# Two batches' scores in one turn of TensorE, two batches' outputs and states in another, and the score tiles' diagonals moved from GpSimd to ScalarE

## The chip, the cores and the metric

One core of a Trainium2 chip runs the whole program. The engines are TensorE (PE; its weight loads are PEld), VectorE (DVE), ScalarE (ACT), GpSimd (POOL) and SyncE (SP), which here issues nearly all DMAs. The metric is the device time of one execution in microseconds (us); lower is better.

## The reference

```python
B, H, S, D = 4, 8, 768, 48
for t in range(S):
    kt, vt, rt = k[:, :, t], v[:, :, t], r[:, :, t]
    cur = np.einsum('bhd,bhe->bhde', u[None] * kt, vt)
    y[:, :, t] = np.einsum('bhd,bhde->bhe', rt, state + cur)
    state = w[None, :, :, None] * state + np.einsum('bhd,bhe->bhde', kt, vt)
x = y.transpose(0, 2, 1, 3).reshape(B * S, H * D)          # 3072 tokens x 384
x = (silu(x @ w_gate) * (x @ w_val)) @ w_out               # inner width 1536
h = x @ w_in                                               # inner width 2048
return (h * np.tanh(np.log1p(np.exp(h)))) @ w_out2
```

A decaying linear attention is followed by two feed-forward networks (FFNs). Everything is float32.

## The kernel before, in words

**Blocks, units, places.** The 768 tokens are cut into six blocks j = 0 to 5 of 128 tokens, each for 4 batches b. The first FFN works on all 4 batches of a block at once (512 columns) in units n = 0 to 71; a unit is one block and one slice f of 128 inner features, and has three groups of nine 128x512 matmuls: `gate`, `val` and `out` (the helper on L294 issues them all, as a high part and a low part of each operand). `out` belongs to the unit before. The table `UNITS` gives the order within a unit; from unit 24 on it is "gate fill act val mul tick mine fill out fill tick tick". `act` is ScalarE's silu of `gate` (L723), `mul` VectorE's product with `val` (L727), `hi` ScalarE's rounded copy (L729), `mine` VectorE's remainder (L735). A `tick` is one step of rounding weights: L180 and L228 on ScalarE, L188, L194, L206 and L212 on VectorE, and L234 on VectorE for the first 36 tiles and on GpSimd for the others. A `fill` is a place where a piece of attention work may be put; each unit has three.

**Attention from block 2 on.** For one batch of one block: GpSimd multiplies r by k and by u (`first` L502, `second` L504), VectorE sums it per head (`total`, L510), and GpSimd writes these sums onto the diagonals of the two score tiles (`diag`, L515: two operations on 128x512). GpSimd also scales r and k by powers of the decay (`later`, `sooner`, L477) and the untransposed k (`keys`, L524). TensorE makes the scores (`scores`, L534, 8 matmuls into two PSUM banks), VectorE copies what lies above the diagonal over them into the two score tiles (`mask`, L541). TensorE then makes the output (`out`, L583, 28 matmuls) and the block's contribution to the state (`state`, L616, 8 matmuls); ScalarE and VectorE round the output into x (`hi` L652, `low` L662), ScalarE fades the state (L639) and VectorE adds to it (`sum`, L632). I call such a run of attention matmuls between FFN matmuls a turn. One batch has two turns, one of scores and one of outputs and states.

**What sets the order.** The lists `AHEAD`, `BEGIN`, `STEPS` and `SPREAD` give the parts in order, and `beside` says at which unit a list begins; a `Filler` deals its steps out over the places. The number behind a part says how many batches ahead it is. Units 14 to 18 still round weights that they need at once. Attention of block 2 lies in units 18 to 23, of blocks 3, 4 and 5 beside units 24 to 59. Within one engine the instructions run in program order.

**Buffers.** `ps_mm` has two PSUM banks, taken in turn by `gate` and `val`; so `gate` of a unit waits until `act` of the unit before has read the same bank. `ps_at` has three, taken in turn by scores (two), output (one) and state (one). `apool` holds two batches of r, k, v; the tile `pr` of `first` and `second` exists once, so `first` waits for the `total` of the batch before. The score tiles exist once.

Of the kernel before, what the change touches and what calls it, by code (L numbers as in the profile page):

```python
# [8 lines left out]
F32 = mybir.dt.float32  # L9
# [3 lines left out]
ALU = mybir.AluOpType  # L13
# [3 lines left out]
P = 128  # L17
# [64 lines left out]

EDGE = 352


@with_exitstack
def tile_decay_attention_then_two_ffns(
# [229 lines left out]
    ypool = first.enter_context(tc.tile_pool(name="ypool", bufs=1))  # L317
    epool = first.enter_context(tc.tile_pool(name="epool", bufs=1))
# [89 lines left out]

    scores = [spool.tile([P, NPAIR, CH], F32, name=f"s{g}") for g in range(2)]
    for t in scores:  # L410
        nc.vector.memset(t, 0.0)
    powers = NPAIR * (HALF + 1)
    pw, qw = ypool.tile([P, DM], F32, name="y"), epool.tile([P, DM], F32, name="pr")
    ones = pw[:, powers : powers + HALF]
# [26 lines left out]
    w128 = const.tile([P, NPAIR], F32, name="w128")  # L441
    late = apool.tile([P, 2, ROW], F32, name="rkv_sb")[:, 0, :WIDE]
    late = late.rearrange("p (n t) -> p n t", n=NPAIR)
    second = apool.tile([P, 2, ROW], F32, name="rkv_sb")
    other = second[:, 1, :WIDE].rearrange("p (n t) -> p n t", n=NPAIR)
    second = second[:, 0, :DM]
    tabn = const.tile([P, H, D], F32, name="tabn")
# [63 lines left out]

    def at_diagonal(j, b):

        for g in range(2):
            nc.gpsimd.tensor_tensor(  # L515
                out=scores[g], in0=four(ident),
                in1=at_in[j, b]["sums"][:, g::2, :].to_broadcast([P, NPAIR, CH]), op=ALU.mult,
            )

# [45 lines left out]

    def at_turned(a, b, ps):


        a["turned"] = ps
        todo = [  # L570
            (i, m, state[:, b, i, m * QUAD : (m + 1) * QUAD], a["r"][:, i, :])
            for m in range(3) for i in range(NPAIR)
        ]
        for g, places in enumerate((((0, 0), (1, QUAD)), ((2, 2 * QUAD + PD - D), (1, QUAD + PD - D)))):
            todo += [
                (i, m, a["v"][i // 2][:, i % 2, c : c + QUAD], scores[g][:, i, :])
                for m, c in places for i in range(NPAIR)
            ]
        ends = {(3 * i + m) % 4: n for n, (i, m, _, _) in enumerate(todo)}
        begun_q = set()  # L580
        for n, (i, m, lhsT, rhs) in enumerate(todo):
            c, q = divmod(3 * i + m, 4)
            nc.tensor.matmul(  # L583
                ps[q * QUAD : (q + 1) * QUAD, c, :], lhsT=lhsT, rhs=rhs,
                start=q not in begun_q, stop=ends[q] == n, skip_group_check=True,
            )
            begun_q.add(q)

    def at_mine(j, b):

# [78 lines left out]
    def after(j, b, n):  # L669
# [179 lines left out]
    def unit1(n, fill=nothing, tick=nothing):  # L849
# [52 lines left out]
    for n in range(2, len(units) - NF1):  # L902
        if n in beside:
            fill.flush()
            fill = Filler(*beside[n])
        if n in (2 * PAIRED - 3, 2 * PAIRED - 2):
            ahead = order[EARLY * B + n - 2 * PAIRED + 3]
# [619 lines left out]
```

## Time and profile before

| | |
|---|---|
| median of 3 runs | 910.26 us (909.64 to 912.01) |
| the profiled execution | 911.0 us, of which the span from first to last instruction is 909.3 us |
| TensorE matmul busy | 900.7 us, 99% of the span |
| VectorE, ScalarE, GpSimd busy | 614.9, 435.3, 175.2 us |
| 128x512 matmuls of the FFNs | 0.39 us each by the record, one begun every 0.227 us |

Times in the rows below are counted from the first instruction. A matmul's record is longer than its share of the engine, since the next one begins before it ends; so the step from one start to the next is what counts. An instruction's record on VectorE or GpSimd holds the time in which it stood on the engine, also when it was held up there.

### The profile page before, as it was taken

Reading aid. Unit: us, or ns where it says so; the run is one execution under the profiler, and the core shown is the slowest. Engines: PE = TensorE matmul, PEld = TensorE weight load, DVE = VectorE, ACT = ScalarE, POOL = GpSimd, SP = SyncE. Lnnn points to the kernel's source line nnn. Section 1 sums busy time; section 2 is a strip of 40 time slices with the busy share of each in tenths; the row PEclk is TensorE's granted clock in tenths of the full one; section 3 lists DMA queues with packets and bytes.
Section 4 is the critical chain, followed back from the end, with each engine's and each line's share of the span. In section 5 each row is a group of like instructions: output and inputs, shape, how many; then the busy total and the mean of one; then the engine's idle time right before and its main releaser. Section 6 shows DMA issues by size and latency. Waiting matters only on the chain.

```text
span 909.3 us, 14895 instructions
## 1 busy us (share of the span) xinstructions
PE 900.7 (99%) x5625; PEld 735.0 (81%) x5625; DVE 614.9 (68%) x1108; ACT 435.3 (48%) x867; POOL 175.2 (19%) x162
## 2 busy tenths in 40 slices
PE   9999999999999999999999999999999999999998
PEld 6888887778888878888888888888888888888886
DVE  8898988545778676743224644758876587776587
ACT  5765542323333433421222345756666475665455
POOL 4200103466555555443000100000000000000000
PEclk9999999999999999999999999999999999999999
DMA  8454732425666766541004748977954549645273
GB/s 315 147 152 125 248 120 65 145 102 175 194 219 213 261 205 206 180 149 53 25 0 144 216 139 294 344 253 237 323 191 151 186 151 311 230 142 173 92 232 116
DMA packets 77576, 164.24 MB, mean 181 GB/s; under 512 B 7616, under 2 KB 34624, under 8 KB 77504
## 3 DMA queue, kind: packets, MB, share of 16 engines
q1 hardware_dynamic: 77072, 162.50, 53.7%
q0 software_dynamic: 432, 0.79, 0.5%
q8 instruction: 44, 0.72, 0.3%
q14 instruction: 28, 0.23, 0.1%
HBM read 126.82 MB, written 36.44 MB: 180 GB/s over the span
## 4 chain that ended last, share of the span: by engine, by line
PE 96%; DVE 2%; DMA 0%; ACT 0%; issue 0%; POOL 0%; POOLq 0%; ACTq 0%; DVEq 0%
PE mm L294 40%; PE acc L294 27%; PE at L294 19%; PE at L583 3%; PE at L534 2%; PE mm L534 1%; PE at L560 1%; PE acc L402 1%; PE at L616 1%; PE acc L492 0%; DMA begun<-o 0%; PE at L552 0%; PE at L656 0%; DVE g_lo L735 0%; DVE o L727 0%
## 5 line engine op out<-in xcount | busy, mean ns | idle before, releaser
L294 PE MATMUL mm<-x_hi,w_split 128*128 128x512 f32 x858 | 281.3, 393 | 1.8 <-DVE w_split L234 1.3
L294 PEld LDWEIGHTS mm<-x_hi,w_split 128*128 128x128 f32 x858 | 160.9, 188 | 38.2 <-DVE w_split L234 1.7
L294 PE MATMUL mm<-x_lo,w_split 128*128 128x512 f32 x429 | 167.4, 390 | 0.1
L727 DVE TENSOR_TENSOR o<-mm,o 128x512 f32<-128x512 f32 x72 | 49.7, 690 | 138.0 <-PE mm L294 101.8
L294 PE MATMUL acc<-g_hi,w_split 128*128 128x512 f32 x420 | 141.5, 393 | 0.0
L936 DVE TENSOR_TENSOR g_lo<-g,g_hi 128x512 fp32r<-128x512 f32 x159 | 106.8, 688 | 23.3 <-ACT g_hi L1014 23.0
L729 ACT ACTIVATE g_hi<-o 128x512 fp32r<-128x512 f32 x72 | 45.5, 632 | 130.1 <-DVE o L727 129.7
L294 PE MATMUL acc<-g_hi,v 128*128 128x512 f32 x288 | 105.1, 389 | 0.0
L1014 ACT ACTIVATE g_hi<-g 128x512 fp32r<-128x512 f32 x159 | 96.1, 623 | 18.3 <-PE at L294 16.3
L936 DVE TENSOR_TENSOR g<-g,at 128x512 f32<-128x512 f32 x72 | 49.5, 688 | 71.3 <-PE at L294 42.7
L294 PEld LDWEIGHTS mm<-x_lo,w_split 128*128 128x128 f32 x429 | 80.6, 188 | 16.4 <-DVE x_lo L662 0.4
L294 PEld LDWEIGHTS acc<-g_hi,w_split 128*128 128x128 f32 x420 | 78.8, 188 | 17.5 <-ACT g_hi L729 0.2
L294 PE MATMUL acc<-g_lo,w_split 128*128 128x512 f32 x210 | 82.2, 391 | 0.3 <-DVE g_lo L735 0.3
L723 ACT ACTIVATE o<-mm 128x512 f32<-128x512 f32 x71 | 42.1, 593 | 81.4 <-PE mm L294 66.5
L1213 ACT ACTIVATE g<-g 128x512 f32<-128x512 f32 x72 | 45.5, 632 | 70.2 <-DVE g L936 69.1
L735 DVE TENSOR_TENSOR g_lo<-o,g_hi 128x512 fp32r<-128x512 f32 x72 | 53.9, 749 | 23.7 <-ACT g_hi L729 23.7
L936 DVE TENSOR_TENSOR g<-g 128x512 f32<-128x512 f32 x96 | 64.5, 686 | 2.7 <-ACT g L1213 2.6
L294 PEld LDWEIGHTS acc<-g_hi,v 128*128 128x128 f32 x288 | 54.1, 188 | 11.2
L294 PE MATMUL at<-g_hi,v 128*128 128x512 f32 x192 | 59.6, 389 | 0.0
L294 PE MATMUL acc<-g_lo,v 128*128 128x512 f32 x144 | 56.0, 389 | 0.0
L294 PE MATMUL mm<-b_hi,w_split 128*128 128x512 f32 x144 | 52.1, 389 | 0.0
L294 PE MATMUL at<-b_hi,w_split 128*128 128x512 f32 x144 | 52.1, 389 | 0.0
(170 smaller groups left out, 1499.3 us busy)
## 6 DMA issues: line engine op xcount, KB each, us to landing
w_raw<-w SPq DMA_DIRECT2D x68, 384.0 KB, 3.5
w_split<-w2s SPq DMA_DIRECT2D x48, 384.0 KB, 5.1
rkv_sb<-rkv_t SPq DMA_DIRECT2D x16, 768.0 KB, 5.0
v<-w2a SPq DMA_DIRECT2D x24, 512.0 KB, 4.0
v<-w2b SPq DMA_DIRECT2D x24, 512.0 KB, 3.6
w_split<-w2z SPq DMA_DIRECT2D x24, 384.0 KB, 5.0
n_sb<-rk_n SPq DMA_DIRECT2D x16, 384.0 KB, 5.6
v<-w2c SPq DMA_DIRECT2D x16, 384.0 KB, 3.7
```

The source lines that it names most:

```text
L294: nc.tensor.matmul(acc, lhsT=wt[:, i, sl], rhs=rhs, start=start, stop=stop, skip_group_check=goes_on)
L402: nc.tensor.matmul(idle, lhsT=mask, rhs=mask.rearrange("p (o t) -> p o t", o=1).to_broadcast([P, 4, CH]), start=True, stop=True,)
L534: nc.tensor.matmul(ps[g][:, i, :], lhsT=a["k"][q, i, :], rhs=a["r"][q, i, :], start=True, stop=True,)
L560: nc.tensor.matmul(ps[t, h * D : (h + 1) * D], lhsT=scores[h % 2][:, h // 2, t], rhs=a["v"][:, h, :], start=(j == 0 and h == heads[0]), st ...
L583: nc.tensor.matmul(ps[q * QUAD : (q + 1) * QUAD, c, :], lhsT=lhsT, rhs=rhs, start=q not in begun_q, stop=ends[q] == n, skip_group_check=True,)
L723: nc.scalar.activation(sg, ps, AF.Silu)
L727: nc.vector.tensor_tensor(out=sg, in0=ps, in1=sg, op=ALU.mult)
L729: nc.scalar.activation(hi, sg, AF.Copy)
L735: eng.tensor_tensor(out=lo, in0=sg, in1=f32(hi), op=ALU.subtract)
L936: nc.vector.tensor_tensor(out=o, in0=a, in1=b, op=op)
L1014: nc.scalar.activation(hi, src, AF.Copy)
L1213: nc.scalar.activation(t, t if src is None else src, AF.Mish)
```

## The change

From block 3 on, batches go in pairs. A list `PAIR` of 18 places (six units) holds the two batches' work: `pair` makes the scores of both in one turn (16 matmuls; the first of the four banks is taken from `ps_mm`, since `ps_at` has three), `outs` makes both outputs and then both states in one turn, with one bank for both states. The two batches have score tiles of their own (`masked`). `apool` holds three batches, with room made by a smaller scratch for DMA descriptors, by dropping `ypool` and by using its tiles for the first blocks' y. The diagonals are written by ScalarE, four 128x128 operations with a scale per row for a score tile, in place of one GpSimd operation; this holds for block 2 too, whose batches still go one by one. `AHEAD` and `BEGIN` are rewritten: what block 2's second batch needs is written behind the scores of the first.

```diff
-SPREAD = [
-    "out state load2 diag1", "hi fade keys1", "low", "sum first2", "scores1 second2",
-    "mask1", "total2 later2 sooner2",
+PAIR = [
+    "pair", "odd", "mask1 first2", "second2", "total2 later2", "sooner2", "",
+    "outs load3", "hi hi1 keys2", "low fade", "low1 fade1 first3 load4",
+    "sum second3 deven2", "sum1 later3 dodd2", "total3 sooner3", "keys3", "deven3", "dodd3", "",
 ]
+LAST = ["first2 second2", "total2 later2 sooner2"]
+FIRST = ["deven2", "dodd2 keys2"]
 AHEAD = [
-    [(2, 0, "first second")], [(2, 0, "total later sooner")], [(2, 0, "diag keys")],
-    [(2, 1, "first second")], [(2, 1, "total later sooner")],
+    [(2, 0, "first second")], [(2, 0, "total later sooner")], [(2, 0, "diag")], [(2, 0, "keys")], [],
 ]
-BEGIN = [[(2, 0, "scores")], [(2, 0, "mask")]]
+BEGIN = [
+    [(2, 0, "scores"), (2, 1, "first second later sooner")], [(2, 0, "mask"), (2, 1, "total")],
+]
...
-    apool = first.enter_context(tc.tile_pool(name="apool", bufs=2))
+    apool = first.enter_context(tc.tile_pool(name="apool", bufs=3))
...
+    def at_diagonal(j, b, gs=range(2)):
+
+        for g in gs:
+            for i in range(NPAIR):
+                nc.scalar.activation(
+                    masked[b % 2][g][:, i, :], ident, AF.Copy,
+                    scale=at_in[j, b]["sums"][:, 2 * i + g, :],
+                )
...
+    def at_pair(j, b):
+
+        at_scores(j, b, (ps_mm, "mm"))
+        at_scores(j, b + 1)
+        at_mask(j, b, [0])
+
+    def at_outs(j, b):
+
+        for i in range(2):
+            at_out(j, b + i)
+        if j + 1 < NJ:
+            ps = ps_at.tile([P, 2, NPAIR, D], F32, name="at")
+            for i in range(2):
+                at_state(j, b + i, ps[:, i])
...
-    beside.update({12 * j - 12: (at_steps(j, SPREAD), 34) for j in range(3, NJ)})
+    rest = [[(2, B - 1, step)] for step in FIRST]
+    for pair in order[3 * B :: 2]:
+        rest += [[(*pair, step)] for step in PAIR]
+    beside[24] = (rest, len(rest))
```

The line numbers of the kernel shift by the change; in the pieces below the changed kernel's L188, L236, L525, L669, L682, L757 and L763 are the old L180, L228, the new diagonals, and the old L639, L652, L723 and L729. "x4" behind a row counts operations of one kind in a row, and "waits" names the engines whose semaphores the row waits for.

On ScalarE, from the silu's `hi` of unit 15 to that of unit 16, there stood before (`o<-mm` is the silu, `w_split<-w_num` the last operation of a tick):

```order
L729 ACTIVATE g_hi<-o 128x512 [waits DVE_49]
L180 ACTIVATE w_num<-w_raw 128x384 [waits DMAHW2_49]
L228 ACTIVATE w_split<-w_num 128x384 [waits DVE_49,PE_49]
L723 ACTIVATE o<-mm 128x512 [waits DMAHW5_49,PE_49]
L729 ACTIVATE g_hi<-o 128x512 [waits DVE_49]
```

and there stands after the change:

```order
L763 ACTIVATE g_hi<-o 128x512 [waits DVE_49]
L188 ACTIVATE w_num<-w_raw 128x384 [waits DMAHW4_49]
L236 ACTIVATE w_split<-w_num 128x384 [waits DVE_49,PE_49]
L525 ACTIVATE s_268<-ident,bonus 128x128 x4
L525 ACTIVATE s_269<-ident,bonus 128x128 x4
L757 ACTIVATE o<-mm 128x512 [waits DMAHW7_49,PE_49]
L763 ACTIVATE g_hi<-o 128x512 [waits DVE_49]
```

The eight diagonals of batch (2, 0) now stand between the tick's last operation and the silu of unit 16.

On ScalarE in unit 18, around the first output of block 2 (`x_hi<-at` is its `hi`, `state<-state` the fade), there stood before:

```order
L180 ACTIVATE w_num<-w_raw 128x384 [waits DMAHW1_49,Activation_49]
L228 ACTIVATE w_raw<-w_num 128x384 [waits DVE_49]
L652 ACTIVATE x_hi<-at 128x3x128 [waits PE_49]
L639 ACTIVATE state<-state,w_293 128x96 x4
L723 ACTIVATE o<-mm 128x512 [waits PE_49]
```

and there stands after the change:

```order
L188 ACTIVATE w_num<-w_raw 128x384 [waits DMAHW3_49,Activation_49]
L236 ACTIVATE w_raw<-w_num 128x384 [waits DVE_49]
L525 ACTIVATE s_270<-ident,bonus 128x128 x4
L525 ACTIVATE s_271<-ident,bonus 128x128 x4
L682 ACTIVATE x_hi<-at 128x3x128 [waits PE_49]
L669 ACTIVATE state<-state,w_294 128x96 x4
L757 ACTIVATE o<-mm 128x512 [waits PE_49]
```

The eight diagonals of batch (2, 1) now stand behind the tick and ahead of the `hi` of batch (2, 0).

On GpSimd, from `later` and `sooner` of batch (2, 0) on (`s<-ident,bonus` is a diagonal, `n_sb<-n_sb,tabn` is `keys`, `pr<-n_sb` is `first`), there stood before:

```order
L477 TENSOR_TENSOR rkv_sb<-rkv_sb,tab 128x512 [waits DMAHW1_49]
L477 TENSOR_TENSOR rkv_sb<-rkv_sb,tab 128x512
L515 TENSOR_TENSOR s_271<-ident,bonus 128x512 [waits DVE_49,PE_49]
L515 TENSOR_TENSOR s_272<-ident,bonus 128x512 [waits PE_49]
L524 TENSOR_TENSOR n_sb<-n_sb,tabn 128x384
L502 TENSOR_TENSOR pr<-n_sb 128x384 [waits DMAHW6_49,Pool_49]
L504 TENSOR_TENSOR pr<-pr,u_sb 128x384 [waits Pool_49]
L477 TENSOR_TENSOR rkv_sb<-rkv_sb,tab 128x512 [waits DMAHW5_49,PE_49]
L477 TENSOR_TENSOR rkv_sb<-rkv_sb,tab 128x512
L515 TENSOR_TENSOR s_271<-ident,bonus 128x512 [waits DVE_49,PE_49]
L515 TENSOR_TENSOR s_272<-ident,bonus 128x512 [waits DVE_49,PE_49]
```

and there stands after the change:

```order
L486 TENSOR_TENSOR rkv_sb<-rkv_sb,tab 128x512 [waits DMAHW1_49]
L486 TENSOR_TENSOR rkv_sb<-rkv_sb,tab 128x512
L534 TENSOR_TENSOR n_sb<-n_sb,tabn 128x384
L511 TENSOR_TENSOR pr<-n_sb 128x384 [waits DMAHW6_49,DVE_49]
L513 TENSOR_TENSOR pr<-pr,u_sb 128x384 [waits Pool_49]
L486 TENSOR_TENSOR rkv_sb<-rkv_sb,tab 128x512 [waits DMAHW5_49,PE_49]
L486 TENSOR_TENSOR rkv_sb<-rkv_sb,tab 128x512
L534 TENSOR_TENSOR n_sb<-n_sb,tabn 128x384
L511 TENSOR_TENSOR pr<-n_sb 128x384 [waits DMAHW2_49,DVE_49]
L513 TENSOR_TENSOR pr<-pr,u_sb 128x384 [waits Pool_49]
```

The diagonals, which waited for TensorE, are gone. So `keys` follows at once, and `first` of batch (2, 1) and of batch (2, 2) wait for nothing later than the `total` of the batch before.

## Rows read from the trace of the kernel before

**Rows 1.** The page: busy time, share and instructions of each engine

```profile
PE 900.7 (99%) x5625; PEld 735.0 (81%) x5625; DVE 614.9 (68%) x1108; ACT 435.3 (48%) x867; POOL 175.2 (19%) x162
```

**Rows 2.** Waits of TensorE: waiter <- awaited: us in total, times, longest

```profile
PE mm L294 <- DVE w_split L234: 1.3, 1, 1.3
```

**Rows 3.** TensorE's timeline, one scores turn: start, us, line, operation, shapes, count

```profile
204.57 1.16 PE L534 MATMUL at<-rkv_sb 48*128 48x128 f32 x16
...
204.78 0.95 PE L534 MATMUL at<-rkv_sb 48*128 48x128 f32 x14
...
205.45 0.28 PE L534 MATMUL at<-rkv_sb 48*128 48x128 f32 x2
205.66 0.50 PE L294 MATMUL acc<-g_hi,w_split 128*128 128x512 f32 x1
...
209.65 0.39 PE L294 MATMUL mm<-x_hi,w_split 128*128 128x512 f32 x1
```

**Rows 4.** TensorE's timeline, the turn of output and state that follows

```profile
209.97 0.86 PE L583 MATMUL at<-rkv_sb,state 128*32 128x128 f32 x24
...
211.30 0.40 PE L583 MATMUL at<-s,rkv_sb 128*32 128x128 f32 x8
211.63 0.56 PE L616 MATMUL at<-rkv_sb,n_sb 128*48 128x48 f32 x16
212.13 0.50 PE L294 MATMUL mm<-x_hi,w_split 128*128 128x512 f32 x1
...
214.33 0.40 PE L294 MATMUL acc<-g_hi,w_split 128*128 128x512 f32 x1
...
220.24 0.39 PE L294 MATMUL mm<-x_hi,w_split 128*128 128x512 f32 x1
```

**Rows 5.** Timeline of units 15 and 16: VectorE, GpSimd, ScalarE, TensorE

```profile
135.05 0.55 DVE L510 TENSOR_REDUCE bonus<-pr 128x8 f32<-128x384 f32 x1
137.79 1.52 DVE L735 TENSOR_TENSOR g_lo<-o,g_hi 128x512 fp32r<-128x512 f32 x1 [0.70 <-ACT g_hi L729]
141.23 3.16 POOL L477 TENSOR_TENSOR rkv_sb<-rkv_sb,tab 128x512 f32<-128x512 f32 x2
145.60 0.58 ACT L723 ACTIVATE o<-mm 128x512 f32<-128x512 f32 x1
146.23 0.50 PE L294 MATMUL mm<-x_hi,w_split 128*128 128x512 f32 x1 [0.56 <-ACT o L723]
```

**Rows 6.** Timeline of units 18 and 19 around the first output of block 2

```profile
158.53 1.36 DVE L541 COPY_PREDICATED s<-mask,at 128x512 f32<-128x512 uint16 x2
161.87 0.69 DVE L735 TENSOR_TENSOR g_lo<-o,g_hi 128x512 fp32r<-128x512 f32 x1 [0.70 <-ACT g_hi L729]
163.77 2.48 POOL L515 TENSOR_TENSOR s<-ident,bonus 128x512 f32<-128x512 f32 x2 [19.38 <-DVE w_split L234]
163.95 1.40 DVE L212 SCALAR_TENSOR_TENSOR w_num<-w_raw,w_num 128x384 uint32<-128x384 uint32 x1
165.81 0.47 ACT L652 ACTIVATE x_hi<-at 128x384 fp32r<-128x384 f32 x1
166.32 0.56 DVE L662 TENSOR_TENSOR x_lo<-at,x_hi 128x384 fp32r<-128x384 f32 x1 [0.97 <-ACT x_hi L652]
168.85 1.16 PE L534 MATMUL at<-rkv_sb 48*128 48x128 f32 x16
```

**Rows 7.** GpSimd's timeline where VectorE has no tick: `first`, then `later` and `sooner`

```profile
171.83 1.02 POOL L502 TENSOR_TENSOR pr<-n_sb 128x384 f32<-128x384 f32 x1 [4.60 <-DMA n_sb<-rk_n]
173.90 2.52 POOL L477 TENSOR_TENSOR rkv_sb<-rkv_sb,tab 128x512 f32<-128x512 f32 x2
```

**Rows 8.** ScalarE's timeline: four 128x128 copies with a scale per row

```profile
6.72 1.28 ACT L452 ACTIVATE rkv_sb<-tab,w 128x128 f32<-128x128 f32 x4 [2.90 <-DVE w L450]
```

**Rows 9.** Timeline in a unit of block 3's stage: a silu, and TensorE's next `gate`

```profile
339.68 0.58 ACT L723 ACTIVATE o<-mm 128x512 f32<-128x512 f32 x1
343.09 0.50 PE L294 MATMUL mm<-x_hi,w_split 128*128 128x512 f32 x1
```

More of the change, by code (lines that the diff above doesn't have):

```diff
@@ L46 @@
 STEPS = [
-    "out state load2 diag1", "hi low fade sum keys1", "scores1 first2 second2",
+    "out state load3 diag1", "hi low fade sum keys1", "scores1 first2 second2",
     "mask1 total2 later2 sooner2",
 ]
-SPREAD = [
-    "out state load2 diag1", "hi fade keys1", "low", "sum first2", "scores1 second2",
-    "mask1", "total2 later2 sooner2",
-]
+PAIR = [
[3 rows of a table added]
+]
+LAST = ["first2 second2", "total2 later2 sooner2"]
+FIRST = ["deven2", "dodd2 keys2"]
 KEYS = [[(1, b, "keys")] for b in range(B)]
@@ L83 @@
 EDGE = 352
+SCRATCH = 4096
 @with_exitstack
@@ L407, in tile_decay_attention_then_two_ffns @@
     warm(12)
-    scores = [spool.tile([P, NPAIR, CH], F32, name=f"s{g}") for g in range(2)]
+    masked = [
+        [spool.tile([P, NPAIR, CH], F32, name=f"s{i}{g}") for g in range(2)] for i in range(2)
+    ]
+    scores = masked[0]
     for t in scores:
         nc.vector.memset(t, 0.0)
+    late, second, third = (apool.tile([P, 2, ROW], F32, name="rkv_sb") for _ in range(3))
+    late = late[:, 0, :WIDE].rearrange("p (n t) -> p n t", n=NPAIR)
+    other = second[:, 1, :WIDE].rearrange("p (n t) -> p n t", n=NPAIR)
+    own = [third[:, 0, :DM], second[:, 0, :DM]]
     powers = NPAIR * (HALF + 1)
-    pw, qw = ypool.tile([P, DM], F32, name="y"), epool.tile([P, DM], F32, name="pr")
+    pw, qw = own[0], epool.tile([P, DM], F32, name="pr")
     ones = pw[:, powers : powers + HALF]
@@ L441, in tile_decay_attention_then_two_ffns @@
     w128 = const.tile([P, NPAIR], F32, name="w128")
[L442 to L446, printed above, removed]
     tabn = const.tile([P, H, D], F32, name="tabn")
@@ L510, in at_own @@
             nc.vector.reduce_sum(out=a["sums"], in_=bonus.pop((j, b)), axis=AX.X)
[L512 to L518, printed above, removed]
+    def at_diagonal(j, b, gs=range(2)):
[5 more added lines that the diff above has]
+                )
     def at_keys(j, b):
@@ L524, in at_keys, with at_scores @@
             eng.tensor_tensor(out=kn, in0=kn, in1=tabn, op=ALU.mult)
-    def at_scores(j, b):
+    def at_scores(j, b, first=None):
         a = at[j, b]
-        pool, name = (ps_mm, "mm") if j < EARLY else (ps_at, "at")
-        ps = a["scores"] = [pool.tile([P, 4, CH], F32, name=name) for _ in range(2)]
+        pools = [(ps_mm, "mm") if j < EARLY else (ps_at, "at")] * 2
+        if first:
+            pools[0] = first
+        ps = a["scores"] = [pool.tile([P, 4, CH], F32, name=name) for pool, name in pools]
         for i in range(NPAIR):
@@ L540, in at_mask @@
         for g in gs:
-            nc.vector.copy_predicated(out=scores[g], mask=mask3, data=at[j, b]["scores"][g])
+            to = scores if j < EARLY else masked[b % 2]
+            nc.vector.copy_predicated(out=to[g], mask=mask3, data=at[j, b]["scores"][g])
+    def at_pair(j, b):
[9 more added lines that the diff above has]
+                at_state(j, b + i, ps[:, i])
     def at_out(j, b):
@@ L547, in at_out @@
         if j >= EARLY:
-            return at_turned(a, b, ps[:, :DM].rearrange("p (c t) -> p c t", c=KC))
+            return at_turned(a, b, ps[:, :DM].rearrange("p (c t) -> p c t", c=KC), masked[b % 2])
         if j:
@@ L564, in at_out, with at_turned @@
                 )
-    def at_turned(a, b, ps):
+    def at_turned(a, b, ps, masks):
         a["turned"] = ps
@@ L575, in at_turned @@
             todo += [
-                (i, m, a["v"][i // 2][:, i % 2, c : c + QUAD], scores[g][:, i, :])
+                (i, m, a["v"][i // 2][:, i % 2, c : c + QUAD], masks[g][:, i, :])
                 for m, c in places for i in range(NPAIR)
@@ L591, in at_mine @@
         a = at[j, b]
-        y = a["y"] = second if b % 2 else ypool.tile([P, DM], F32, name="y")
+        y = a["y"] = own[b % 2]
         sums = epool.tile([P, H], F32, name="bonus")
@@ L602, in at_y, with at_state @@
         nc.vector.tensor_tensor(out=a["y"], in0=a["out"][:, :DM], in1=a["y"], op=ALU.add)
-    def at_state(j, b):
+    def at_state(j, b, ps=None):
         if j + 1 == NJ:
@@ L607, in at_state @@
         a = at_in[j, b]
-        if j == 0:
+        if ps is not None:
+            pass
+        elif j == 0:
             ps = ps_acc.tile([P, NPAIR, D], F32, name="acc2")
@@ L682, in tile_decay_attention_then_two_ffns @@
         "mask": at_mask,
-        "even": lambda j, b: at_mask(j, b, [0]),
+        "pair": at_pair,
         "odd": lambda j, b: at_mask(j, b, [1]),
+        "outs": at_outs,
         "diag": at_diagonal,
+        "deven": lambda j, b: at_diagonal(j, b, [0]),
+        "dodd": lambda j, b: at_diagonal(j, b, [1]),
         "load": lambda j, b: (at_tiles(j, b), load_at(j, b)),
@@ L694, in at_part @@
     def at_part(j, b, part):
-        name = part.rstrip("12")
+        name = part.rstrip("1234")
         to = after(j, b, int(part[len(name) :] or 0))
@@ L699, in at_part, with at_steps @@
             PARTS[name](*to)
-    def at_steps(j, steps):
-        return [[(j, b, step)] for b in range(B) for step in steps]
+    def at_steps(j):
+        steps = [[(j, b, step)] for b in range(B) for step in STEPS]
+        return steps[:-2] + [[(j, B - 1, step)] for step in LAST]
     def do(step):
@@ L905, in tile_decay_attention_then_two_ffns @@
             fill = Filler(*beside[n])
[L906 removed]
+        if n in (2 * PAIRED - 3, 2 * PAIRED - 2, 2 * PAIRED - 1):
             ahead = order[EARLY * B + n - 2 * PAIRED + 3]
```

5 lines of the change are left out of this document (2 added, 3 removed).

## Prediction

> **What bounds the kernel now.** I read the page first. TensorE is busy for 99% of the span [rows 1], so time can only come from work that leaves TensorE or from gaps between its matmuls. Then the waits: the longest is one of 1.3 us for a weight [rows 2]; the other that matters here is 0.56 us for a silu [rows 5]. Waits are no more than that. So I looked at what the waits don't count: the steps between matmul starts in TensorE's timeline, around a turn of attention [rows 3, 4].
>
> In a run of FFN matmuls one begins every 0.227 us (214.33 to 220.24, 26 steps) [rows 4]. A turn of scores costs more than its own matmuls in three spots. The step into a turn is 0.32 us (209.65 to 209.97) [rows 3, 4], 0.09 over the pace. Inside, six of eight scores matmuls take 0.67 us (204.78 to 205.45), 0.112 each, so eight are worth 0.90; from 204.57 to 205.66 it is 1.09, 0.19 more. And behind it 17 steps take 3.99 us (205.66 to 209.65) against 3.86, 0.13 more [rows 3]. That is 0.41 us for a turn, whatever is in it. For outputs and states [rows 4]: 0.09 on the way in; 24 of 28 output matmuls take 1.33 us (209.97 to 211.30), so 28 are worth 1.55, and from 209.97 to 211.63 it is 1.66, 0.11 more; 35 steps behind it take 8.11 us against 7.95, 0.16 more. The 0.50 us of the eight state matmuls has such a share too, which no row here divides; I take 0.1, between nothing and 0.2. Together 0.46 us.
>
> **What the change takes away.** Blocks 3, 4 and 5 have 12 batches, so 12 turns of scores become 6, and 12 of outputs become 6. Six turns of scores saved are 6 x 0.41 = 2.5 us. Four output turns with states (blocks 3 and 4) are 4 x 0.46 = 1.8, two without states (block 5) 2 x 0.36 = 0.7. The matmuls stay, and block 2 keeps its eight turns. Sum: **-5.0 us**. The bounds are 4.6 (no share in the states) and 5.4.
>
> **What it adds: the diagonals on ScalarE.** Four 128x128 operations take 1.28 us, about 0.30 for each further one [rows 8], so a batch's eight take 2.4 us. ScalarE has the time (435.3 us busy) [rows 1], but it works in order, and what stands behind the diagonals waits. In two places the order puts them ahead of something that TensorE needs.
>
> First, unit 16. The silu now stands behind batch (2, 0)'s diagonals, and these behind the tick that VectorE works on from 137.79. That tick is slow in the trace: VectorE's remainder takes 1.52 us there and 0.69 at 161.87, and GpSimd's two scalings 3.16 us there and 2.52 elsewhere [rows 5, 6, 7]. So I take it that here the two take turns. GpSimd now has five operations behind the `total` that ends at 135.60: three of 1.02 us and two that take 2.52 together [rows 5, 7], 5.6 us without the diagonals. Of these, 2.1 are done by 137.79, so 3.5 remain to be shared with VectorE's six operations, 2.6 us when undisturbed (five from 161.87 to 163.95, and half a microsecond) [rows 6]. 137.79 + 3.5 + 2.6 = 143.9, then 0.5 for ScalarE's end of the tick, 2.4 for the diagonals, 0.6 for the silu: 147.4, where it ended at 146.18 [rows 5]. That is 1.2 us later for unit 17's `gate`, which waits for that bank. The 1.3 us wait for a weight two groups on [rows 2] gets shorter by some 0.3, since the `total` of batch (2, 1) leaves VectorE's queue there. Net **+0.9**; bounds -0.6 (the wait of 0.56 us goes) and +2.4 (the whole block of diagonals).
>
> Second, units 18 and 19, the larger. The scores of batch (2, 1) at 168.85 take the bank that VectorE's `low` of batch (2, 0) must have read; it ended at 166.88, 2 us early [rows 6]. `low` waits for ScalarE's `hi`, which now stands behind the diagonals of (2, 1), which stand behind a tick. In the trace that tick is free of GpSimd until 163.77, because GpSimd waits there for TensorE with its diagonals [rows 6]. After the change GpSimd waits for the `total` only, which follows the masks (they end at 159.89) and 0.55 more [rows 5, 6]: its five operations of batch (2, 2) begin at 160.5, on top of the tick. At 161.87 there remain 4.2 of 5.6 us; taking turns with all but the last two VectorE operations (1.8 of 2.6 us) ends at 167.9, and the last two at 168.7. Then 0.5 for ScalarE's end of the tick, 2.4 of diagonals, 0.5 of `hi`, 0.56 of `low`: 172.7, and the scores' second matmul stands until then. **+3.7 us**. The bounds: nothing (tick undisturbed, ending at 164.5, `low` at 168.5) and 4.4.
>
> The Trainium skill (SBUF — State Buffer, section "SBUF: two separate sides") says that VectorE and GpSimd take a shared pair of ports as an exclusive lock for a whole instruction, and that the other one blocks. The stretched 1.52 and 3.16 us agree. By an even split of a port's bandwidth, against which the page speaks, VectorE's 2.6 us would take 5.2, end at 167.1, and the stall would be 2.1 in place of 3.7.
>
> **Costed at nothing.** The first bank of a pair's scores comes from `ps_mm`, so the next unit's `val` waits for that mask: a mask takes 0.7 us [rows 6], and the second batch's scores (0.9) and nine `gate` matmuls (2.0) lie between; without that cover it would be 0.7 and a hand-over, six times. The third buffer of `apool` lets loads go a batch earlier. The smaller scratch touches only three accumulating DMAs late in the first FFN, whose readers come units later. Ticks stay as they are, and GpSimd is not on the path from unit 24 on.
>
> **Sum.** -5.0 + 0.9 + 3.7 = -0.4 us on an execution of 911.0, whose span is 909.3. That execution lies 0.7 above the median of the runs, 910.26, so I put the change to the median: **909.9 us**.
>
> **Rivals.**
> *The two holds do not come.* GpSimd's operations of (2, 1) and (2, 2) fall elsewhere, VectorE's ticks run undisturbed, and the diagonals end in time. Then the whole saving stays: -5.0 and perhaps the 0.56 us [rows 5]: 905.0. For it speaks that the second hold has 2 us of slack now and needs most of the disturbance worked out above; against it that the disturbance is plain [rows 5], and that nothing but the `total` keeps GpSimd back.
> *Slower: diagonals in front of the silu beside units 24 to 59.* There too ScalarE works a batch's eight operations between a tick and a silu. In one such unit the silu ends at 340.26 and the `gate` that needs its bank begins at 343.09 [rows 9]: 2.8 us to spare, of which a block of diagonals takes 2.4, and the fewer turns leave TensorE less to do in between. It decides where a silu is more than 0.4 us later than in that unit. If half of the 12 blocks cost 0.8 us each, that is 4.8 over my sum: 914.7. Against it: GpSimd has no diagonals then and gets its work in single places, so ticks should end earlier.
> *The change does not save what it says.* If the fixed share of a turn comes with the change of operands inside it, as from one batch to the next, a joined turn costs as two. Then the holds remain: 914.8. Against it: inside a turn the pace is even from head to head [rows 3].
>
> **Chances.** What tells a change here is 0.3%, 2.7 us: faster is below 907.5, slower above 913.0. Likeliest (holds as worked out) 0.55, own range 907.0 to 912.1 (the second hold between 1.7, with half of the disturbance, and 4.4, the first between 0 and 2.4); no holds 0.30, around 905; late silus 0.12; nothing saved 0.03. Of the likeliest I give 0.02 to each side. So faster 0.32, same 0.51, slower 0.17. The range that leaves 2 in 10 out reaches to the no-hold case and stops short of the late silus: 904.3 to 912.3.
>
> **What would show it.** Right: 12 turns fewer in TensorE's timeline beside units 24 to 59, joined scores turns near 2.0 us and the matmuls from unit 24 to 59 some 5 us shorter in all; a wait of TensorE for `low` near 169 us of 3 to 4 us, and one for a silu near 146 us of 1.5 to 2; VectorE's operations stretched behind 161.87. Wrong: `low` of (2, 0) done before its scores (then 905), or waits for silus, of the order of 1 us, that come back every six units (then over 913). A joined turn that still costs 0.4 us for each batch would break the first term.

## The result, and the profile after

| | median | runs |
|---|---|---|
| before | 910.25 us (909.64 to 912.01) | 6 |
| after | 915.66 us (914.13 to 917.72) | 6 |
| ratio | 1.0058, 95% interval 1.0044 to 1.0071 | |
| predicted | 909.9 us, range 904.3 to 912.3 | |

Slower by 5.4 us, outside the range. The profiled execution of after took 916.11 us, its span is 914.4. Line numbers of after are 8 to 34 higher than before: L234 is now L242, L294 L302, L534 L546, L652 L682, L662 L692, L723 L757, L727 L761, L735 L769, L477 L486, L502 L511, L524 L534; ScalarE's diagonals are L525.

The page of after, busy time by engine:

```profile
PE 899.5 (98%) x5625; PEld 736.3 (81%) x5625; DVE 607.6 (66%) x1108; ACT 471.3 (52%) x995; POOL 139.1 (15%) x130
```

Beside [rows 1] this is the change as written: GpSimd 36 us less, ScalarE 36 more, TensorE's instructions the same in number. The waits of TensorE in after (waiter <- awaited: us in total, times, longest):

```profile
PE mm L302 <- ACT o L757: 3.0, 5, 1.2
PE at L546 <- DVE x_lo L692: 2.6, 1, 2.6
...
PE mm L302 <- DVE w_split L242: 0.9, 1, 0.9
...
PE mm L546 <- POOL w_raw L242: 0.6, 1, 0.6
```

Before, the longest behind the opening was the 1.3 of [rows 2]; one of 1.4 us for a mask of GpSimd's stands in the opening of both kernels. Now silus (L757) hold TensorE five times, and `low` (L692) once for 2.6 us.

To see where the 5.1 us between the spans come from, I matched the n-th FFN matmul of one trace with the n-th of the other (3528 in each) and took the difference of their starts:

| stretch of after, us | after later than before by, at its end | within it |
|---|---|---|
| 0 to 112 | 0.28 | +0.28 |
| 112 to 120 | 0.92 | +0.64 |
| 134 to 148 | 1.61 | +0.69 |
| 148 to 169 | 1.25 | -0.36 |
| 169 to 178 | 5.92 | +4.67 |
| 206 to 460 | 5.11 | -0.81 |
| 460 to the end | 5.11 | 0 |

TensorE's timeline of after (start, us, line, operation, shapes, count; in brackets the wait that the profile shows ahead of it), at the places of these steps:

```profile
117.34 0.39 PE L302 MATMUL at<-g_hi,w_split 128*128 128x512 f32 x1
118.08 0.50 PE L302 MATMUL at<-g_lo,w_split 128*128 128x512 f32 x1 [0.35 <-DVE g_lo L769]
...
146.03 0.56 PE L646 MATMUL at<-w_split 128*48 128x48 f32 x16
147.84 0.50 PE L302 MATMUL mm<-x_hi,w_split 128*128 128x512 f32 x1 [1.25 <-ACT o L757]
...
170.09 0.48 PE L546 MATMUL at<-rkv_sb 48*128 48x128 f32 x2
173.17 1.16 PE L546 MATMUL at<-rkv_sb 48*128 48x128 f32 x14 [2.59 <-DVE x_lo L692]
...
174.80 0.63 PE L302 MATMUL acc<-g_lo,w_split 128*128 128x512 f32 x1
175.23 1.05 PE L302 MATMUL acc<-g_hi,w_split 128*128 128x512 f32 x2
...
218.65 0.37 PE L546 MATMUL mm<-rkv_sb 48*128 48x128 f32 x1
...
220.63 0.50 PE L302 MATMUL mm<-x_hi,w_split 128*128 128x512 f32 x1
...
235.14 0.86 PE L611 MATMUL at<-rkv_sb,state 128*32 128x128 f32 x24
...
239.19 0.50 PE L302 MATMUL mm<-x_hi,w_split 128*128 128x512 f32 x1
...
257.59 0.50 PE L302 MATMUL mm<-x_hi,w_split 128*128 128x512 f32 x1 [0.67 <-ACT o L757]
```

**The turns did what they were to do.** Joined scores take 1.98 us (218.65 to 220.63), where two turns of [rows 3] take 2.18; two outputs and two states 4.05 (235.14 to 239.19) against 4.32 by [rows 4], and the steps into and behind a turn come once.

**The second hold is there, and something behind it.** The scores of batch (2, 1) stop for 2.59 us; in [rows 6] they ran through. Then FFN matmuls begin 0.427 us apart (174.80 to 175.23) in place of 0.227. The windows before and after that moment (us, busy time and count of PE, PEld, DVE, ACT, POOL, then the granted clock of TensorE, DMA share, GB/s):

```profile
170.00:174.30 4.30, 1.71 (x18) 1.30 (x17) 1.23 (x3) 4.07 (x14) 0.00 (x0) 1.00 0.87 286
174.30:177.80 3.50, 3.50 (x10) 2.74 (x10) 2.06 (x5) 1.23 (x2) 0.00 (x0) 0.51 0.19 71
```

The granted clock is 0.51 there, the lower of the two levels (1.2 GHz), right after TensorE stood for 2.6 us. Of the 4.67 us, the longer scores turn is 3.07 (4.16 for 1.09) and the slow matmuls 1.60.

VectorE, ScalarE and GpSimd around it:

```profile
164.24 1.43 DVE L196 TENSOR_SCALAR w_num<-w_num 128x384 f32<-128x384 f32 x1
...
168.71 0.55 DVE L220 SCALAR_TENSOR_TENSOR w_num<-w_raw,w_num 128x384 uint32<-128x384 uint32 x1
172.56 0.56 DVE L692 TENSOR_TENSOR x_lo<-at,x_hi 128x384 fp32r<-128x384 f32 x1 [3.30 <-ACT x_hi L682]
...
169.29 0.53 ACT L236 ACTIVATE w_raw<-w_num 128x384 fp32r<-128x384 f32 x1 [5.78 <-DVE w_num L220]
169.72 2.43 ACT L525 ACTIVATE s<-ident,bonus 128x128 f32<-128x128 f32 x8
172.06 0.46 ACT L682 ACTIVATE x_hi<-at 128x384 fp32r<-128x384 f32 x1
...
161.66 1.02 POOL L511 TENSOR_TENSOR pr<-n_sb 128x384 f32<-128x384 f32 x1 [18.93 <-DVE bonus L519]
...
166.78 1.33 POOL L534 TENSOR_TENSOR n_sb<-n_sb,tabn 128x384 f32<-128x384 f32 x1
```

This is the chain of the prediction: GpSimd's five operations from 161.66 to 168.1 (the first starts right behind the `total`, L519, as its bracket says), VectorE's tick from 164.24 to 169.26, then the diagonals, then `hi`, then `low`, which ends at 173.12.

**From unit 24 on the saving is mostly eaten.** Between a pair's outputs and the next scores lie 99 FFN matmuls, which take 22.67 us undisturbed. In after the first four of the five such stretches take 24.79 (from 239.19), 24.67, 22.94 and 23.61: 5.3 us too much. The longest one, in units 27 to 30, on ScalarE, VectorE and GpSimd:

```profile
244.25 0.85 ACT L682 ACTIVATE x_hi<-at 128x384 fp32r<-128x384 f32 x2
244.99 1.17 ACT L669 ACTIVATE state<-state,w 128x96 f32<-128x96 f32 x4
247.35 0.57 ACT L188 ACTIVATE w_num<-w_raw 128x384 f32<-128x384 f32 x1 [1.19 <-POOL pr L511]
...
248.22 1.16 ACT L669 ACTIVATE state<-state,w 128x96 f32<-128x96 f32 x4
249.28 0.59 ACT L757 ACTIVATE o<-mm 128x512 f32<-128x512 f32 x1
...
254.62 2.44 ACT L525 ACTIVATE s<-ident,bonus 128x128 f32<-128x128 f32 x8
256.96 0.58 ACT L757 ACTIVATE o<-mm 128x512 f32<-128x512 f32 x1
...
241.62 0.69 DVE L761 TENSOR_TENSOR o<-mm,o 128x512 f32<-128x512 f32 x1 [7.63 <-issue]
...
251.77 1.65 DVE L202 SCALAR_TENSOR_TENSOR w_num<-w_raw,w_num 128x384 uint32<-128x384 uint32 x1
...
250.34 2.66 POOL L486 TENSOR_TENSOR rkv_sb<-rkv_sb,tab 128x512 f32<-128x512 f32 x2
```

The outputs of a pair stand between unit 27's `gate` and its `val`, 4.05 us in one piece, so unit 27's product (L761) comes only at 241.62, and its tick and the two x_hi follow it. Unit 27 has two ticks. The second tick and two batches' fades then stand ahead of unit 28's silu, which begins at 249.28, though its `gate` was done near 245.3 (27 matmuls of 0.227 us after 239.19). One tick later, slowed by GpSimd's scalings (1.65 us for L202), come eight diagonals and a silu at 256.96, for which TensorE waits until 257.59. The same happens six units on, where unit 33 has two ticks. These two stretches hold 4.1 of the 5.3 us. Of the rest, 0.3 lies in the third and 0.9 in the fourth, most of it ahead of the scores at 396 us, whose first bank a silu must have read:

```profile
396.19 0.57 ACT L757 ACTIVATE o<-mm 128x512 f32<-128x512 f32 x1
...
396.86 0.34 PE L546 MATMUL mm<-rkv_sb 48*128 48x128 f32 x1 [0.62 <-POOL w_raw L242]
```

The bracket names GpSimd, which was done at 396.21; the silu ended at 396.76, 0.10 us ahead of the scores.

### The profile page after: what moved, and what is told of

It reads as the page before. It is cut to its first block, busy times and chain, and to the rows that moved or that the text cites. A ratio compares the mean times of both kernels' runs of the same rounds, so it can differ in the third digit from the quotient of the medians.

```text
span 914.4 us, 14959 instructions
## 1 busy us (share of the span) xinstructions
PE 899.5 (98%) x5625; PEld 736.3 (81%) x5625; DVE 607.6 (66%) x1108; ACT 471.3 (52%) x995; POOL 139.1 (15%) x130
## 2 busy tenths in 40 slices
DMA packets 77577, 164.24 MB, mean 180 GB/s; under 512 B 7616, under 2 KB 34624, under 8 KB 77504
## 4 chain that ended last, share of the span: by engine, by line
PE 92%; DVE 3%; ACT 2%; DMA 1%; issue 1%; SPq 0%; POOL 0%; DVEq 0%; POOLq 0%; ACTq 0%
PE mm L302 38%; PE acc L302 25%; PE at L302 19%; PE at L611 3%; PE mm L546 2%; PE at L546 1%; DMA w2s<-w_raw 1%; ACT s L525 1%; DVE w_num L202 1%; PE at L588 1%; PE acc L409 1%; PE at L646 1%; DVE w_num L196 1%; PE acc L501 0%; DVE w_num L220 0%
## 5 line engine op out<-in xcount | busy, mean ns | idle before, releaser
L302 PE MATMUL mm<-x_hi,w_split 128*128 128x512 f32 x858 | 281.5, 394 | 3.9 <-ACT o L757 3.0
L302 PEld LDWEIGHTS mm<-x_hi,w_split 128*128 128x128 f32 x858 | 161.0, 188 | 42.5 <-ACT o L757 5.5
L302 PE MATMUL mm<-x_lo,w_split 128*128 128x512 f32 x429 | 167.5, 391 | 0.1
L761 DVE TENSOR_TENSOR o<-mm,o 128x512 f32<-128x512 f32 x72 | 49.8, 691 | 146.2 <-PE mm L302 97.6
L302 PE MATMUL acc<-g_hi,w_split 128*128 128x512 f32 x420 | 141.4, 393 | 0.0
L763 ACT ACTIVATE g_hi<-o 128x512 fp32r<-128x512 f32 x72 | 45.5, 632 | 129.4 <-DVE o L761 129.1
L302 PE MATMUL acc<-g_hi,v 128*128 128x512 f32 x288 | 105.1, 389 | 0.0
L302 PEld LDWEIGHTS mm<-x_lo,w_split 128*128 128x128 f32 x429 | 80.6, 188 | 16.1 <-DVE x_lo L692 0.4
L302 PEld LDWEIGHTS acc<-g_hi,w_split 128*128 128x128 f32 x420 | 79.6, 190 | 16.8
L302 PE MATMUL acc<-g_lo,w_split 128*128 128x512 f32 x210 | 82.9, 395 | 0.9 <-DVE g_lo L769 0.9
L757 ACT ACTIVATE o<-mm 128x512 f32<-128x512 f32 x71 | 41.9, 590 | 66.6 <-PE mm L302 55.2
L769 DVE TENSOR_TENSOR g_lo<-o,g_hi 128x512 fp32r<-128x512 f32 x72 | 51.8, 720 | 23.7 <-ACT g_hi L763 23.7
L302 PEld LDWEIGHTS acc<-g_hi,v 128*128 128x128 f32 x288 | 54.1, 188 | 11.3
L302 PE MATMUL at<-g_hi,v 128*128 128x512 f32 x192 | 59.6, 389 | 0.0
L302 PE MATMUL acc<-g_lo,v 128*128 128x512 f32 x144 | 56.0, 389 | 0.0
L302 PE MATMUL at<-b_hi,w_split 128*128 128x512 f32 x144 | 52.1, 389 | 0.0
L302 PE MATMUL mm<-b_hi,w_split 128*128 128x512 f32 x144 | 52.1, 389 | 0.0
```

The costliest lines, as they stand in the source:

```text
L302: nc.tensor.matmul(acc, lhsT=wt[:, i, sl], rhs=rhs, start=start, stop=stop, skip_group_check=goes_on)
L757: nc.scalar.activation(sg, ps, AF.Silu)
L761: nc.vector.tensor_tensor(out=sg, in0=ps, in1=sg, op=ALU.mult)
L763: nc.scalar.activation(hi, sg, AF.Copy)
L769: eng.tensor_tensor(out=lo, in0=sg, in1=f32(hi), op=ALU.subtract)
```

## The experiments

The question was which part of the change brings the waits: theory O, ScalarE's order (diagonals, x_hi and fades ahead of what TensorE needs); rival P, the joined turns themselves; rival G, GpSimd stretching VectorE's ticks. For the half clock: that it follows the second hold, or has a cause of its own.

All times beside the kernel before on the same chip; before was 910.26 (first four), 910.16 (next three) and 910.24 (last). The columns on the right come from matching FFN matmuls as above, profiled execution against before, in us: the opening (to 112), 112 to 169, the stretch of the second hold, and units 24 on.

| kernel | median us | ratio, 95% interval | opening | 112-169 | hold | from 24 on |
|---|---|---|---|---|---|---|
| after | 915.66 | 1.0058, 1.0044 to 1.0071 | +0.28 | +0.97 | +4.67 | -0.81 |
| e1_pool_diag | 919.32 | 1.0106, 1.0092 to 1.0120 | -0.14 | -0.19 | +2.36 | +4.5 |
| e2_act_alone | 913.53 | 1.0049, 1.0030 to 1.0068 | -0.12 | +1.04 | 0.00 | +1.4 |
| e3_hi_first | 911.14 | 1.0013, 1.0005 to 1.0022 | +0.30 | +1.02 | +0.70 | -1.2 |
| e4_ticks_apart | 911.09 | 1.0010, 1.0001 to 1.0019 | -0.09 | +1.01 | +4.65 | -6.1 |
| e5_both | 906.76 | 0.9965, 0.9953 to 0.9978 | -0.81 | +0.99 | +0.77 | -5.4 |
| e6_both_first | 906.01 | 0.9949, 0.9935 to 0.9963 | +1.80 | -0.77 | +0.71 | -5.5 |
| e7_pool_apart | 912.30 | 1.0019, 1.0009 to 1.0029 | -0.67 | -0.19 | +3.91 | -1.7 |
| e8_last_half | 904.69 | 0.9942, 0.9928 to 0.9955 | -1.78 | -0.80 | +0.72 | -5.3 |

Line numbers of e1_pool_diag and e7_pool_apart are one lower than those of after behind the diagonals, those of e2_act_alone one higher than those of before. No edit touches the opening; that a single execution differs by up to 1.8 us there is chance, and has to be taken off before profiled times are compared.

**e1_pool_diag.** The diagonals back to GpSimd, everything else as in after:

```diff
-            for i in range(NPAIR):
-                nc.scalar.activation(
-                    masked[b % 2][g][:, i, :], ident, AF.Copy,
-                    scale=at_in[j, b]["sums"][:, 2 * i + g, :],
-                )
+            nc.gpsimd.tensor_tensor(
+                out=masked[b % 2][g], in0=four(ident),
+                in1=at_in[j, b]["sums"][:, g::2, :].to_broadcast([P, NPAIR, CH]), op=ALU.mult,
+            )
```

> The changed kernel with the diagonals given back to GpSimd (two operations a batch, at the same places, into the same two sets of masks); the joined turns stay. Theory O (ScalarE's order: diagonals, and x_hi and fades beside them, stand ahead of a silu or of hi): the waits of 0.7 to 1.1 us in units 27 to 36 and the one of 1.0 at 396 us go, 5.2 us in units 24 to 59; hi of batch (2, 0) is not behind diagonals, so the hold at 170 us falls from 2.9 to under 1 and the half clock behind it (1.6) does not come. Sum about -8, of which GpSimd's longer chain may take back 1 to 2: 907 to 909 us. Rival P (the joined turns themselves cost it: banks, two batches' x_hi and fades at once): units 24 to 59 keep at least 4 of the 5.2 us, and the time is 911 to 914. Rival G (GpSimd stretching VectorE's ticks is what costs): with 1.8 us more of GpSimd a batch the waits grow, and the time is 916 or more.

Slower still, by 3.7 us. Theory O falls in the form in which I had it: diagonals ahead of silus are not the cause by themselves. What after had lost at 117 and at 146 us is gone, so those two losses do come with the diagonals' move. The hold at 170 us, for which O had under 1 us, stays at 1.8 us of waiting: no diagonals stand ahead of `hi` here, but GpSimd's longer chain ends the tick at 169.3 as in after, and TensorE, not delayed before, is there 1.6 us earlier. TensorE's timeline and GpSimd's in unit 29:

```profile
250.21 0.39 PE L302 MATMUL acc<-g_hi,w_split 128*128 128x512 f32 x1
252.51 0.50 PE L302 MATMUL acc<-g_lo,w_split 128*128 128x512 f32 x1 [1.92 <-DVE g_lo L768]
...
250.06 1.38 POOL L486 TENSOR_TENSOR rkv_sb<-rkv_sb,tab 128x512 f32<-128x512 f32 x1
```

GpSimd now works without a break from 244.44 to 251.4, and VectorE's four operations of the tick take 5.55 us in all (1.8 undisturbed), so TensorE waits 1.9 us for `g_lo`. From unit 24 on rival G's forecast came true for this kernel; that GpSimd's stretching alone is what costs in after does not follow from it (see e4_ticks_apart).

**e2_act_alone.** The kernel before, with the loop of ScalarE (the lines marked - above) in place of GpSimd's operation, into the one set of score tiles, and nothing else.

> The kernel before with one thing of the change: the diagonals by ScalarE, eight a batch, at their places of before (single turns, one set of masks, loads of before). Theory O: the hold at 169 us comes here too, 2.5 to 3.5 us and the half clock behind it 1.6, and the one at 146 us, 0.4 to 1; beside units 24 to 59 some of the silus are late, 0 to 4 us. Slower than the kernel before by 4 to 9: 914 to 919 us. Rival P (the pairs carry the cost): within 1.5 us of the kernel before, 909 to 912.

Slower than before by 3.3 us, more than rival P allowed and less than O. Of what O had listed, the hold at 146 us came (+0.70, as in after), and 1.4 us beside units 24 to 59; +0.64 at 117 us came as in after, without being on its list; the largest, the second hold, did not come in the profiled execution. ScalarE and TensorE there:

```profile
165.46 0.53 ACT L228 ACTIVATE w_raw<-w_num 128x384 fp32r<-128x384 f32 x1 [2.27 <-DVE w_num L212]
165.89 2.44 ACT L516 ACTIVATE s<-ident,bonus 128x128 f32<-128x128 f32 x8
168.24 0.46 ACT L653 ACTIVATE x_hi<-at 128x384 fp32r<-128x384 f32 x1
...
169.77 1.16 PE L535 MATMUL at<-rkv_sb 48*128 48x128 f32 x16
```

The diagonals stand ahead of `hi` here too, but GpSimd is idle (its next batch is not loaded before 172 us), the tick ends at 165.5 instead of 169.3, and `low` ends at 169.3, in time. So the second hold of after is made of both: the tick stretched by GpSimd (3.8 us) and the diagonals (2.4). The diagonals alone hold nothing here; a stretched tick alone holds TensorE for 0.24 us in e3_hi_first, and for 1.8 us in e1_pool_diag, where TensorE is there earlier. In two of the six executions the mean granted clock is 0.996 and 0.995 (917.7 and 917.9 us), in the others 0.999 to 1.000; whether the second hold came in those two no trace shows.

**e3_hi_first.**

```diff
-    "out state load3 diag1", "hi low fade sum keys1", "scores1 first2 second2",
+    "out state load3", "hi low fade sum keys1", "diag1 scores1 first2 second2",
```

> The changed kernel with block 2's diagonals two steps later, behind hi and low of the batch before. If the hold at 170 us is hi behind the diagonals, and the half clock is what follows TensorE's standing still: the gap goes from 2.87 to about 0.6 (the tick in front of hi still ends late, 169.3), and the stretch at half clock goes with it: -2.3 - 1.6 = -3.9, 911.8 us. If the clock falls there for another reason: -2.3 only, 913.4, and eight matmuls of 0.427 us still stand behind the scores. If hi is late for GpSimd's sake alone, the gap stays over 2 and the time within 1 us of 915.7.

-4.5 us. TensorE's timeline, then the window behind it:

```profile
170.17 0.49 PE L546 MATMUL at<-rkv_sb 48*128 48x128 f32 x2
170.90 1.16 PE L546 MATMUL at<-rkv_sb 48*128 48x128 f32 x14 [0.24 <-DVE x_lo L692]
```

```profile
174.00:177.70 3.70, 3.70 (x63) 2.98 (x65) 2.99 (x5) 1.83 (x5) 0.00 (x0) 1.00 0.54 203
```

The tick still ends at 169.35, but `hi` follows it at once; the standing is 0.24 us and the clock stays at its upper level. All 11 executions have a mean granted clock of 0.999 or 1.000, where those of after have 0.995 to 0.998. The clock's fall was a consequence of the hold.

**e4_ticks_apart.**

```diff
+        due += {26: 0.4, 27: -0.4, 32: 0.4, 33: -0.4}.get(n, 0)
         due += 2.17 if n < 2 * PAIRED else 2 if n == ready - 2 else 1 if n < ready else 0 if n < 24 else 1.3
```

> The changed kernel with the second tick of units 27 and 33 moved one unit earlier (to 26 and 32), so that the units with a pair's outputs, x_hi and fades have one tick. If two ticks and the pair's x_hi and fades together make the silus late there: the waits behind units 27 and 33 (0.62, 0.68 and 1.06 us, and 0.55, 0.64 and 1.06) fall to under a third, -2.5 to -3.5 us: 912 to 913. Rival: the diagonals behind the tick that GpSimd's scalings stretch make them, whatever the number of ticks: the pair of 1.06 stays and so does the g_lo wait, at most -1: 914.7 to 916.

More than expected: all the waits behind units 27 and 33 go, and the first two stretches of 99 matmuls take 22.67 us. The fourth does too: the wait ahead of a pair's scores, which the edit doesn't touch, is gone in this trace and back in e5_both (0.92 us from start to start); why stays open. ScalarE in unit 28:

```profile
244.64 2.23 ACT L669 ACTIVATE state<-state,w 128x96 f32<-128x96 f32 x8
246.77 0.58 ACT L757 ACTIVATE o<-mm 128x512 f32<-128x512 f32 x1
...
251.78 2.44 ACT L525 ACTIVATE s<-ident,bonus 128x128 f32<-128x128 f32 x8
254.12 0.58 ACT L757 ACTIVATE o<-mm 128x512 f32<-128x512 f32 x1
```

The same x_hi, fades and diagonals stand in the same order, and GpSimd stretches the same tick; but without the second tick the silus come 2.5 and 2.8 us earlier (0.35 of it since the whole stretch begins earlier, at 238.84), and TensorE doesn't wait. In this execution the clock fell behind the second hold as in after.

**e5_both.** The edits of e3_hi_first and e4_ticks_apart together.

> The changed kernel with both single edits that each took 4.5 us off it: block 2's diagonals behind hi and low, and the second tick in units 26 and 32. If the two losses are separate (one beside units 18 and 19, one beside units 27 to 37), the gains add: 915.7 - 4.5 - 4.5 = 906.7, faster than the kernel before by 3.5. If one cause stands behind both (for instance the clock, or DMA that shifts), they don't add: 909 to 911.

The gains add: 906.76 us, for 906.7. This is the first version that beats the kernel before.

**e6_both_first.** On top of e5_both:

```diff
-    [(2, 0, "first second")], [(2, 0, "total later sooner")], [(2, 0, "diag")], [(2, 0, "keys")], [],
+    [(2, 0, "first second")], [(2, 0, "total deven later sooner")], [(2, 0, "dodd")], [(2, 0, "keys")], [],
...
-            eng = nc.vector if j == 1 else nc.gpsimd
+            eng = nc.vector if j == 1 or (j, b) == (2, 0) else nc.gpsimd
```

> e5_both with two more edits for the first two small losses: keys of batch (2, 0) by VectorE at its place instead of GpSimd, which ran it at 115 us beside a tick (the wait of 0.73 at 117 us should become 0.23, -0.5), and half of batch (2, 0)'s diagonals one tick earlier (the silu of unit 16 1.2 us earlier, the gap of 1.46 at 146 us becomes 0.76 as in the kernel before, -0.7; the weight wait at 155 us may give back 0.3). 905.5 to 906.2. If the gaps at 117 and 146 us have nothing to do with keys and the diagonals, it is e5_both's time.

At 112 to 169 us it stands 1.76 us better than e5_both: the gap at 117 us is gone, and that at 146 us wholly, with the 0.56 of [rows 5] too. In the medians that is 0.75 us, inside the intervals.

**e7_pool_apart.** The edits of e1_pool_diag and e4_ticks_apart together.

> The changed kernel with the diagonals on GpSimd (as e1_pool_diag, 919.3) and the second tick in units 26 and 32. If GpSimd's diagonals cost because they stretch VectorE's tick, and two ticks with the pair's x_hi and fades make the tick late to begin with: the g_lo waits of 2.3 us fall, but not to nothing, as they do with the diagonals on ScalarE: 912 to 916. If the joined turns alone cost it (the diagonals' engine doesn't matter): the time of e4_ticks_apart, 911.1, plus or minus 1.

-7.0 us against e1_pool_diag. By the traces units 24 on gain 6.2 (+4.5 to -1.7), and the second hold loses 1.55, since the clock fell behind it this time. But 4.4 us of waits remain from unit 24 on that e4_ticks_apart, with ScalarE's diagonals, doesn't have. So once the ticks lie apart, ScalarE is the better place for the diagonals beside units 24 to 59. The medians differ by 1.2 us only, because GpSimd's diagonals spare the waits at 117 and 146 us (1.2 us) and the second hold is shorter (0.7).

**e8_last_half.** On top of e6_both_first:

```diff
-    "sum second3 deven2", "sum1 later3 dodd2", "total3 sooner3", "keys3", "deven3", "dodd3", "",
+    "sum second3 deven2", "sum1 later3 dodd2", "total3 sooner3", "keys3", "deven3", "", "dodd3",
```

> e6_both_first with the last four diagonals of a pair (odd heads of its second batch) one place later, behind the silu of the unit in which the next pair's scores stand, instead of ahead of it. The first bank of a pair's scores is the one that this silu reads (the wait of 0.84 us at 387 us, and 0.39 at 344); with 1.2 us less in front of it the silu is done before the scores: -0.6 to -0.8, 905.2 to 905.4. If that bank is held by something else, no change: 906.0.

The wait ahead of a pair's scores goes, as expected, but another silu is late: the step ahead of a `gate` is 0.67 us in place of 0.23, six microseconds earlier, which the trace shows as

```profile
378.19 0.50 PE L302 MATMUL mm<-x_hi,w_split 128*128 128x512 f32 x1 [0.28 <-ACT o L757]
```

and by the traces units 24 on gain nothing (-5.5 and -5.3). The medians differ by 1.3 us, with overlapping intervals; what of that is real stays open. It is the fastest version: 5.6 us below the kernel before, 11.0 below the change as it was made.

## Why the prediction was wrong

**Turns saved: -5.0 forecast, 6.1 found.** From unit 24 on after gains 0.81 net, with 5.3 lost to waits; e4_ticks_apart, almost without waits there, gains 6.1. A pair with states saves 1.00 us by the lengths of turns and of the FFN runs behind them, four times, one without 0.83, twice; and two scores turns of before had been stretched by 0.26 each, which no longer happens. The term was right in kind and a fifth too small.

**First hold: +0.9 forecast, +0.33 found** (+0.69, and -0.36 from the weight wait). The silu ended at 147.79 for a forecast 147.4; TensorE was 0.92 us late by then, so that against TensorE's work the silu was half a microsecond earlier than forecast.

**Second hold: +3.7 forecast, 3.07 found,** by the chain forecast, and both its links are shown: without GpSimd's stretch (e2_act_alone) it is nothing, without the diagonals ahead of `hi` (e3_hi_first) the step is 0.52 us in place of 2.87. What the sum lacked is the 1.60 us of half clock behind it. The forecast had VectorE and GpSimd take turns for whole operations (3.7), against an even split of a port (2.1); 3.07 lies between. VectorE's operations of 0.35 and 0.55 us took 1.43 and 1.64 beside GpSimd's, about one of GpSimd's scalings each (3.09 for two). The exclusive lock of which the Trainium skill (SBUF — State Buffer, section "SBUF: two separate sides") tells would look like that.

**The step that failed is "Costed at nothing": "Ticks stay as they are, and GpSimd is not on the path from unit 24 on."** It cost 5.3 us, 4.1 of them behind units 27 and 33. I had priced the joined turn by what TensorE saves, and had not asked what is behind it: outputs of 4.05 us in one piece delay the unit's `val`, its product and its tick, and two batches' x_hi and fades (3.2 us of ScalarE) come at once behind that. In the two units in which a second tick falls into this, the silu begins 4 us after its `gate` is done. GpSimd, which I took to be off the path, by the profile's bracket holds up ScalarE's first operation of the second tick (1.19 us, at 247.35 above) and stretches the next tick, and eight diagonals close the chain. That the second tick is needed for it is shown by e4_ticks_apart; that the length of the turn is, I read from the trace, since no run has shorter output turns with everything else alike. The rival "Slower" gave this place and nearly this price (4.8 us), but a part of the cause only, the diagonals, and it got 0.12; what was argued against it, that GpSimd without diagonals would leave the ticks alone, did not hold (1.65 us for L202 at 251.77). The sign of being wrong that went with it, waits for silus of the order of 1 us every six units, is what came (1.06 us from start to start at 257.59, and again six units on).

**Two smaller ones were not seen.** Before, batch (2, 0)'s diagonals held GpSimd until its `total` was there, and `keys` came behind them, at 137.74. Rid of them, GpSimd ran these `keys` beside a tick. Its rows of before, then of after:

```profile
135.74 2.05 POOL L515 TENSOR_TENSOR s<-ident,bonus 128x512 f32<-128x512 f32 x2 [20.55 <-DVE bonus L510]
...
115.41 1.33 POOL L534 TENSOR_TENSOR n_sb<-n_sb,tabn 128x384 f32<-128x384 f32 x1
```

That is +0.64 at 117 us, gone when VectorE does it (e6_both_first). And of the bank that a pair's scores take from `ps_mm` I looked at the next reader; its last one, a silu, is what the scores at 396 us wait for (1.01 us from start to start in after; this is a part of the 5.3).

The sum as found: 0.28 - 6.1 + 0.33 + 0.64 + 4.67 + 5.3 = 5.1 us, the difference of the spans.

## What to carry to other kernels

A longer turn on the busiest engine is also a longer pause for everything fed by its other work: before joining turns, follow what was to run beside the old, shorter ones, and look for the unit in which all of it falls together. An instruction moved off an engine also frees that engine to run ahead, to wherever its next buffer allows; ask which neighbour it then disturbs. When a change loses, look first for the few units that lose: two lines of order turned 5.4 us lost into 3.4 gained.

## What the runs showed of the hardware that was not expected

TensorE's clock fell to the lower level behind a single hold in a kernel in which it is otherwise busy all the time, and not each time: with a step of 2.87 us between two matmul starts it fell in both kernels that had one (after, e4_ticks_apart); with the same scores turn standing 1.84 us in e1_pool_diag and in e7_pool_apart it fell in the second only:

```profile
171.80:175.00 3.20, 3.20 (x9) 2.45 (x8) 2.11 (x4) 1.12 (x2) 0.00 (x0) 0.51 0.84 324
```

In e1_pool_diag, two waits for `g_lo` of 1.92 and 1.91 us, six units apart, left the clock alone the first time and halved it the second:

```profile
249.00:255.00 6.00, 4.08 (x19) 3.02 (x18) 5.90 (x10) 1.01 (x2) 4.94 (x5) 1.00 0.72 262
...
299.30:302.60 3.30, 3.30 (x9) 2.55 (x8) 3.22 (x6) 1.09 (x2) 3.26 (x4) 0.50 0.82 238
```

These two steps are 2.30 us from start to start, the two at the scores 2.12. No shorter step from 112 us on was followed by a fall in any of the traces (the longest are 2.02 us in e1_pool_diag and 1.87 in e7_pool_apart). What decides between the two cases the runs don't show. A hold of 2 to 2.3 us is thus to be priced with about 1.6 us more as a chance, 8 matmuls of 0.427 us where 0.227 is the pace.
